# Another written-out order of steps in a fused recurrence and Fourier-mixing kernel

## The chip, the cores and the metric

The kernel runs on one core of one Trainium2 chip. The metric is the device time of the launch in microseconds; of the kernel before it is known from three runs and from one further profiled execution. The engines are named as in the profile: PE (TensorE, matmuls), PEld (its weight loads), DVE (VectorE), ACT (ScalarE), POOL (GpSimd) and SP (SyncE, here the issuer of nearly all DMAs). PSUM is the memory that PE writes.

## What is computed

Two blocks follow one another. The first is a gated linear recurrence over 768 tokens for 4 batches of 8 heads of width 48. The second mixes each batch's 768 x 384 matrix by a two-dimensional Fourier transform, normalises it, and passes it through two projections with a ReLU between them.

```python
f = 1.0 / (1.0 + np.exp(-f_logit))
for t in range(S):
    state = f[:, :, t, :, None] * state + np.einsum('bhd,bhe->bhde', k[:, :, t], v[:, :, t])
    y[:, :, t] = np.einsum('bhd,bhde->bhe', q[:, :, t], state)
x = y.transpose(0, 2, 1, 3).reshape(B, S, H * D)
u = x + np.real(np.fft.fft(np.fft.fft(x, axis=1), axis=2))
un = (u - mean(u)) / np.sqrt(var(u) + 1e-06)          # over the last axis
out = u + np.maximum(un @ w_ch1, 0.0) @ w_ch2          # 384 -> 1536 -> 384
```

## The kernel before

**Units.** The recurrence is cut into 16 units, one for each batch and pair of heads (`attention`, L316). Unit `u` belongs to batch `u // 4`. Each unit is a generator of 13 or 14 steps:

1. gates: two ACT passes over `g` (L331, L332)
2. the running sum of the log gates on DVE (`W`, L338), with two small operations (L339, and L340 on POOL)
3. three exponentials on ACT (L343, L344, L346)
4. `q` and `k` scaled on DVE (L350, L351)
5. scores `sc` on PE (L362): 24 matmuls on 48x64 tiles of the array, four tiles side by side, into two PSUM tiles
6. the causal mask on DVE (L369, two operations, one for each PSUM tile)
7. transposes `st` of the keys on PE (L507) and their copy `kT` on ACT (L509)
8. the states' increments `ds` on PE (L518, tiled)
9. the scan over chunks on DVE (L526)
10. `y` from the scores on PE (L538, tiled)
11. `y` from the states on PE (L545, tiled) and five copies `yT` on ACT (L554 to L558)
12. transposes `yt` back on PE (L565) and the copy into `x` on ACT (L567)
13. and 14. the fold of tokens and channels for the Fourier transform, on DVE and POOL (L591 to L614); step 14 exists for the last two units of a batch

**Batches.** When its four units are folded, a batch goes through `fnet`: four steps `z` (L652) with copies on ACT, then three steps `mix` (L671) with additions and moments on DVE. A further generator, `turns`, makes the normalised rows `un` (L707), their transposes `pt` (L710) and the copies `unT` (L711). `projected` then runs the first projection `up` (L752, 12 steps for each pair of row blocks, each followed by a ReLU on ACT, L754) and the second one, for the first pair as plain products `po` (L761), for the others as seven products of a Strassen-like scheme, `fx` and `fz` (L775), with additions on DVE (L782 to L809) and the stores of `out` (L619 on POOL's queue, L626 on SP's or ACT's).

**Weights.** The weights come as 64-bit words in 24 blocks. Each is fetched by SP (384 KB, L268), at most three ahead, and brought to single precision by one ACT, two DVE and one POOL operation (L239, L241, L242, L243). Later they are read a second time, and DVE takes each block's smallest size (L302). A last test, `judge`, combines these with the recurrence's extremes into one flag: six small DVE operations (L824 to L829), one matmul `turned` (L831), two more DVE operations (L832, L834). All engines load the flag (L884) and branch on it (L885); where it is set, which it is not for these inputs, everything is computed again in a slower way.

**The order.** No scheduler decides. The string `ORDER` lists 684 words, and each engine gets its instructions in this order, each engine's queue in program order. A number means that unit's next step. `F`, `H` and `P` with a number mean the next step of that batch's `fnet`, `turns` and `projected`. `L` loads gates, keys, queries or values of a unit (`L4fk`), `r` fetches a weight block, `R` three, `C` converts one, `W` makes the sums for the seven products, `V` reads a block again and `c` takes its size, `M` is the test. `D` puts four matmuls of constant data on PE (L154) that keep it occupied. `G` clears the middle rows of a tile, `I`, `i`, `T`, `S`, `Z` set up constants and tables.

**Buffers.** `sc` (two tiles), `st`, `ds` and `yt` share one PSUM pool of two buffers; `z`, `mix`, `pt`, `up`, `po`, `fx` and `fz` share another of two; `y` has one. Gates and keys have three tiles, queries four, values four, raw weight blocks three.

Of the kernel before, what the change touches and what calls it, by code (L numbers as in the profile page):

```python
# [12 lines left out]
C = 128  # L13
# [11 lines left out]


ORDER = (
    "Gq2 r I D Gq0 L0f Gk1 L1f D Gk0 L0q i D Gq3 C Gq1 Z L0k 0 D 1 Gk2 0 L1q 1 L1k D D D D D D D D D D D "
    "D 0 0 1 0 r 1 L2f 0 2 C L1v 1 L3fk 1 3 L0v 0 1 L2q 2 0 0 r 1 L2k 3 1 0 2 r 3 L3q 2 L2v 0 C L3v C "
    "L4fk R 4 2 2 3 1 0 C 2 4 1 3 L5qv D L4qv L5fk 3 D D 3 2 0 2 3 2 3 C r 4 1 4 L6fk C r 2 5 4 L6qv 4 2 "  # L30
    "1 5 6 3 4 D 4 C 5 3 T 3 6 4 5 5 4 2 r L7fk 5 2 D L7qv 3 3 5 7 S L8fk C 4 7 6 6 5 F0 5 r r F0 F0 F0 "
    "7 4 C F0 L9fk 5 6 8 H0 H0 6 5 6 r H0 C L8qv 6 7 L9qv P0 6 7 r C P0 7 7 C 9 P0 r r 5 8 C r C F0 r 7 "
    "F0 6 P0 5 9 C 6 7 P0 r C P0 8 8 C P0 r r 7 P0 P0 8 9 H0 C P0 P0 8 7 8 C P0 H0 7 9 6 H0 H0 C 9 r C "
    "P0 9 L10fk r 9 P0 r C 9 L11fk 10 C 6 6 P0 11 4 P0 P0 P0 P0 P0 P0 10 P0 P0 P0 L10qv P0 P0 7 7 F1 9 "
    "P0 F1 H0 9 W P0 P0 P0 11 F1 P0 L11qv P0 P0 P0 9 P0 P0 P0 8 L12fk P0 11 11 8 P0 P0 10 11 F1 P0 11 11 "
    "10 L14fk F1 8 P0 14 F1 P0 10 P0 8 10 P0 P0 H1 H1 10 L12qv P0 P0 10 P0 F1 P0 11 11 10 P0 10 H1 P0 P0 "
    "P0 P0 12 12 12 P0 P0 12 P0 H1 P0 12 P0 H1 L13fk P1 P1 P1 P1 P1 14 13 P1 12 8 8 P1 P1 12 9 10 L13qv "
    "13 P1 P1 L14qv 9 P1 12 11 P1 H1 11 10 P1 P1 13 P1 13 P1 12 P1 P1 14 P1 14 V 13 P1 c V 10 10 P1 P1 "
    "P1 P1 P1 V L15fk P1 13 P1 11 V P1 P1 P1 P1 c P1 11 11 F2 V c F2 F2 H1 13 H1 F2 c 14 P1 c V c P1 P1 "
    "12 P1 P1 14 P1 P1 13 V V V P1 15 F2 c P1 12 P1 P1 P1 P1 c P1 H2 14 15 V V P1 P1 P1 P1 P1 13 P1 14 "  # L40
    "F2 P1 c P1 P1 15 V 13 P1 H2 P1 P1 L15qv P1 14 13 P1 V 12 H2 F2 14 P2 P2 P2 P2 P2 P2 P2 15 P2 P2 P2 "
    "c c 12 H2 V H2 15 H2 15 P2 c P2 15 P2 P2 15 P2 14 13 15 P2 P2 14 P2 P2 15 13 P2 P2 P2 P2 P2 H2 V 15 "
    "P2 P2 14 14 15 H2 P2 P2 P2 P2 15 15 F3 F3 P2 F3 F3 P2 F3 c P2 P2 P2 P2 P2 V P2 c P2 V c c V P2 P2 "
    "P2 P2 P2 c P2 F3 F3 P2 V P2 H3 P2 P2 P2 H3 H3 P2 P2 P2 P2 P2 P2 P2 P2 P2 P2 P3 H3 c P3 P3 P3 P3 V "
    "P3 c P3 P3 P3 c V V c P3 P3 P3 H3 P3 P3 P3 P3 P3 P3 c P3 P3 V P3 H3 P3 P3 P3 P3 P3 P3 H3 H3 P3 P3 "
    "P3 P3 P3 P3 P3 P3 P3 P3 P3 P3 V P3 P3 P3 P3 P3 c P3 c P3 P3 P3 M P3 P3 P3 P3 P3 P3 P3 P3 P3 P3 P3 "
    "P3"
)

PAIRS = ((0, 3), (2, 5), (1, 4))  # L50
# [4 lines left out]
def kernel(  # L55
# [14 lines left out]
    B, HP, _, D, _, S = qkf.shape  # L70
# [8 lines left out]
    R = 64 + D  # L79
# [417 lines left out]
    def outputs(u, x_all, AT, Q, K, te, T=None):  # L497
# [66 lines left out]
        for c, i in enumerate((0, 1, 4, 2, 3, 5)):  # L564
# [4 lines left out]
            ps[:, :NCH * 128].rearrange("t (c r k) -> t c r k", r=2, k=64)[:, :, :, :D])  # L569
        yield  # L570
        yield from fold(u, x)

    eo_of = {}

    def fold(u, x):

        b, hp = divmod(u, HP)
        if b not in eo_of:
            eo_of[b] = p1.tile([128, 8, DM], F32, tag="eo", name=f"eo{b}")
        eo = eo_of[b] if hp < HP - 1 else eo_of.pop(b)
        ch = slice(hp * 2 * D, (hp + 1) * 2 * D)
        f = eo[:, :, ch]
        last = hp == HP - 1
        other = nc.vector if last else nc.gpsimd  # L590
        other.tensor_tensor(f[:, 6:3:-1], x[:, 0:3, ch], x[:, 3:6, ch], ALU.subtract)  # L591
        nc.vector.tensor_tensor(f[:, 1:4], x[:, 0:3, ch], x[:, 3:6, ch], ALU.add)
        nc.vector.tensor_tensor(f[:, 0:8:7], f[:, 1:7:5], f[:, 2:6:3], ALU.add)
        nc.vector.tensor_tensor(f[:, 2:6:3], f[:, 1:7:5], f[:, 2:6:3], ALU.subtract)
        other.tensor_copy(f[:, 1:7:5], f[:, 0:8:7])
        other.tensor_copy(f[0:1, 0], f[0:1, 2])
        other.tensor_tensor(f[0:1, 2:7:4], x[0:1, 0:2, ch], x[0:1, 3:5, ch], ALU.subtract)
        if hp < HP // 2:
            return
        yield  # L600


        lo, hi = (QD + 1, HD) if hp == HP // 2 else (1, QD + 1)
        up = slice(DM - lo, DM - hi, -1)
        tt = nc.vector.tensor_tensor
        tt(xs[:, :, lo:hi], eo[:, 4:7, lo:hi], eo[:, 4:7, up], ALU.subtract)
        if last:
            tt(se[:, :, 1:QD], xs[:, :, 1:QD], xs[:, :, HD - 1:QD:-1], ALU.subtract)
            tt(xs[:, :, 1:QD + 1], xs[:, :, 1:QD + 1], xs[:, :, HD - 1:QD - 1:-1], ALU.add)
        tt(xc[:, :, lo:hi], eo[:, 0:4, lo:hi], eo[:, 0:4, up], ALU.add)  # L610
        if last:
            nc.vector.tensor_copy(xc[:, :, 0:HD + 1:HD], eo[:, 0:4, 0:HD + 1:HD])
            tt(ce, xc[:, :, 0:QD + 1], xc[:, :, HD:QD - 1:-1], ALU.add)
            tt(xc[:, :, 0:QD], xc[:, :, 0:QD], xc[:, :, HD:QD:-1], ALU.subtract)  # L614
# [362 lines left out]
```

## Time and profile before

| what | value |
|---|---|
| median of 3 runs | 552.56 us (552.45 to 554.12) |
| span of the profiled execution | 551.2 us |
| PE, DVE, ACT, POOL busy | 527.8, 300.1, 192.8, 96.1 us |
| `up` L752 on PE | 864 matmul passes, 197.0 us |
| `fx` and `fz` L775 on PE | 161.8 us in all forms |
| `sc`, `y`, `y`, `ds` (L362, L538, L545, L518) on PE | 26.3, 55.0, 21.4, 32.3 us |
| DMA | 44.38 MB, mean 81 GB/s |

The profiled execution is 1.3 us shorter in its span than the runs' median; the runs' time also counts what lies around the span. PE's busy time counts matmuls that overlap, so it says where PE works and not how fast. A matmul in single precision appears as two passes in the trace, so that `up`'s 12 steps of three matmuls appear as 72 passes. L154, the constant matmuls, take 12.9 us of PE's busy time in the first 65 us.

### The profile page before, as it was taken

To read this page: it belongs to the slowest core of one execution; us is meant where nothing else is said; L and a number is where in the kernel's file an instruction comes from. 1 tells how busy PE (TensorE), PEld (TensorE's weight loads), DVE (VectorE), ACT (ScalarE), POOL (GpSimd) and SP (SyncE) were. 2 spreads that over 40 slices of the span, in tenths; PEclk is the share of its full clock that TensorE was granted. 3 is DMA by queue.
4 is the path that set the end of the run, shared out by engine and by line. 5 is a ranking of instruction groups with operands and counts; after the bars stand their busy time and mean duration, and the time that the engine had idled before them with its cause. 6 is when DMAs were issued, how large, how long until landed. Compare 5 with 4: busy or idle time off the path is not lost.

```text
span 551.2 us, 10204 instructions
## 1 busy us (share of the span) xinstructions
PE 527.8 (96%) x4186; PEld 463.6 (84%) x4186; DVE 300.1 (54%) x534; ACT 192.8 (35%) x497; POOL 96.1 (17%) x147
## 2 busy tenths in 40 slices
PE   7797989999999999999999999999999999999995
PEld 5686768876898889889889899899889798989985
DVE  8999999984936437426644344444452441413231
ACT  5767485771332432551340422321411303021110
POOL 7146535434001000121101001003001000010000
PEclk9888799999999999999999999999999999999999
DMA  8979745353102100412540301002012004000001
GB/s 220 260 212 227 210 136 165 122 175 107 51 0 73 44 1 7 111 44 84 160 115 17 114 1 59 29 1 87 0 30 87 1 14 159 0 30 0 30 2 34
DMA packets 18398, 44.38 MB, mean 81 GB/s; under 512 B 3109, under 2 KB 4710, under 8 KB 18342
## 3 DMA queue, kind: packets, MB, share of 16 engines
q1 hardware_dynamic: 17094, 39.89, 25.9%
q0 software_dynamic: 1104, 3.54, 1.8%
q8 instruction: 35, 0.57, 0.4%
q10 hardware_dynamic: 144, 0.20, 0.1%
q14 instruction: 21, 0.17, 0.1%
HBM read 38.90 MB, written 4.72 MB: 79 GB/s over the span
## 4 chain that ended last, share of the span: by engine, by line
PE 88%; DVE 3%; ACT 3%; DMA 2%; POOL 1%; issue 1%; SPq 0%; ACTq 0%; POOLq 0%
PE up L752 35%; PE fx L775 16%; PE fz L775 12%; PE y L538 4%; PE sc L362 3%; PE z L652 3%; PE y L545 3%; PE po L761 3%; PE mix L671 3%; PE ds L518 2%; PE yt L565 2%; PE st L507 1%; PE pt L710 1%; DMA k<-in_qkf_dram 1%; DMA g<-in_qkf_dram 1%
## 5 line engine op out<-in xcount | busy, mean ns | idle before, releaser
L752 PE MATMUL up<-unT,w 128*128 128x256 f32 x864 | 197.0, 382 | 1.5 <-DVE x L730 0.9
L752 PEld LDWEIGHTS up<-unT,w 128*128 128x128 f32 x864 | 161.0, 190 | 26.1 <-issue 1.5
L754 ACT ACTIVATE h<-up 128x256 f32<-128x256 f32 x144 | 55.2, 383 | 199.4 <-PE up L752 199.4
L619 POOL DMA_INDIRECT out_dram<-x,place x16 | 16.9, 1056 | 270.4 <-DVE x L805 234.0
L775 PE MATMUL fx<-block,h 128*128 128x192 f32 x264 | 46.5, 326 | 0.0
L775 PE MATMUL fx<-w,h 128*128 128x192 f32 x264 | 44.9, 327 | 0.1
L775 PEld LDWEIGHTS fx<-w,h 128*128 128x128 f32 x264 | 43.1, 190 | 0.8 <-ACT h L754 0.4
L775 PEld LDWEIGHTS fx<-block,h 128*128 128x128 f32 x264 | 43.5, 190 | 0.0
L782 DVE TENSOR_TENSOR s<-h,h 128x768 f32<-128x768 f32 x11 | 10.5, 954 | 50.3 <-ACT h L754 50.3
L243 POOL TENSOR_TENSOR w<-w,raw 128x384 uint32<-128x384 uint32 x24 | 28.2, 1178 | 45.8 <-ACT raw L239 25.6
L369 DVE COPY_PREDICATED at<-causal,sc 128x768 f32<-128x768 uint32 x32 | 31.3, 1031 | 0.9 <-PE sc L362 0.8
L362 PE MATMUL sc<-q,W 48*64 48x128 f32 x768 | 26.3, 283 | 5.2 <-issue 3.3
L362 PEld LDWEIGHTS sc<-q,W 48*64 48x64 f32 x768 | 22.1, 138 | 8.9 <-issue 5.4
L338 DVE TENSOR_TENSOR_SCAN W<-g,bound 112x768 f32<-112x768 f32 x16 | 28.4, 1775 | 0.8 <-issue 0.7
L727 DVE TENSOR_TENSOR x<-mix,x 128x384 f32<-128x384 f32 x12 | 6.7, 555 | 39.0 <-PE mix L671 39.0
L538 PE MATMUL y<-at,v 128*64 128x128 f32 (+1 forms) x384 | 27.9, 300 | 0.0
L538 PEld LDWEIGHTS y<-at,v 128*64 128x64 f32 (+1 forms) x384 | 23.9, 143 | 3.2 <-issue 3.2
L775 PE MATMUL fz<-w,s 128*128 128x192 f32 x132 | 23.5, 328 | 0.0
L775 PE MATMUL fz<-block,h 128*128 128x192 f32 x132 | 23.5, 328 | 0.0
L775 PE MATMUL fz<-w,h 128*128 128x192 f32 x132 | 23.4, 327 | 0.0
L775 PEld LDWEIGHTS fz<-w,s 128*128 128x128 f32 x132 | 21.6, 190 | 0.3 <-issue 0.3
L697 ACT ACTIVATE rstd<-mv,eps 128x1 f32<-128x1 f32 (+1 forms) x20 | 5.9, 294 | 45.7 <-DVE mv L694 45.7
(145 smaller groups left out, 750.3 us busy)
## 6 DMA issues: line engine op xcount, KB each, us to landing
raw<-in_w_ch_dram SPq DMA_DIRECT2D x24, 384.0 KB, 4.3
g<-in_qkf_dram SPq DMA_DIRECT2D x32, 144.0 KB, 4.4
q<-in_qkf_dram SPq DMA_DIRECT2D x32, 144.0 KB, 4.1
k<-in_qkf_dram SPq DMA_DIRECT2D x32, 144.0 KB, 4.7
v<-in_v_dram SPq DMA_DIRECT2D x16, 288.0 KB, 5.0
k<-in_w_ch_dram SPq DMA_DIRECT2D x12, 384.0 KB
g<-in_w_ch_dram SPq DMA_DIRECT2D x12, 384.0 KB, 5.2
out_dram<-x SPq DMA_DIRECT2D x4, 168.0 KB
```

The costliest lines, as they stand in the source:

```text
L243: nc.gpsimd.tensor_tensor(bits, bits, lo, ALU.add)
L338: nc.vector.tensor_tensor_scan(W, g, bound[:R], 0.0, ALU.add, ALU.min)
L362: nc.tensor.matmul(ps[64 * s:64 * s + 64, r, i * C:(i + 1) * C], lhsT=W[ROWS[r], o + 64 * s:o + 64 * s + 64], rhs=Q[ROWS[r], o:o + C], sta ...
L369: nc.vector.copy_predicated(AT[:, :, half], causal.bitcast(U32).unsqueeze(1).unsqueeze(1).to_broadcast([128, 2, NCH // 2, C]), ps[:, :, :N ...
L538: nc.tensor.matmul(y[FILL[r], c * C:(c + 1) * C], lhsT=vt[:, c, r * D:r * D + (64 if r == 0 else D)], rhs=AT[:, r, c], start=(c % 4 == 0), ...
L545: nc.tensor.matmul(y[ROWS[r], c * C:(c + 1) * C], lhsT=st[ROWS[r], :, c - 1], rhs=Q[ROWS[r], c * C:(c + 1) * C], start=False, stop=True, s ...
L619: nc.gpsimd.indirect_dma_start(out=out.rearrange("b s d -> (b s) d"), out_offset=bass.IndirectOffsetOnAxis(ap=place[:, b, i:i + 1], axis=0 ...
L652: nc.tensor.matmul(z[:, cols], lhsT=src[:, j, lo:hi], rhs=tab[:, t, T % 2, cols], start=(i == 0), stop=(i == len(parts) - 1), skip_group_c ...
L671: nc.tensor.matmul(mix[:, o], lhsT=zz[:rows_of[T], T, PLACES[c]], rhs=cd[:rows_of[T], T, :NQ - odd], start=(i == 0), stop=(i == 1))
L752: nc.tensor.matmul(pp[:, :256], lhsT=w1[:, kt, m * 128:(m + 1) * 128], rhs=unT[:, kt], start=(kt == 0), stop=(kt == 2))
L754: nc.scalar.activation(hs[-1][:, m % H].rearrange("p t n -> p (t n)"), pp[:, :256], AF.Relu)
L775: nc.tensor.matmul(out, lhsT=h[:, m], rhs=blocks[i][:, m], start=(start and m == 0), stop=(m == H - 1), skip_group_check=True)
```

## The change

The list of words is another one. Each word stands in it as often as before. What differs is their sequence: tiled steps of several units stand next to each other, the first loads and the clearing of tiles come in another order, the weight blocks are fetched and converted at other places, `up` and product steps stand between the units' steps in another way, and the test `M` is the last word, where twelve words `P3` followed it before.

Where the two lists have reached the first `P0`, the word counts are these: the old one has done 11 `C` and the steps of unit 5 up to 11, unit 6 up to 8, unit 7 up to 4 and unit 8 up to 1; the new one has done 8 `C` and the steps of unit 5 up to 12, unit 6 up to 4 and unit 7 up to 3. Units 0 to 3 and unit 4 up to step 12 are done in both, and all 21 `D`.

A second edit keeps a batch's fold buffer in the table until the last step that uses it, so that the last steps of a batch's units may come in another sequence.

The diff, with the list cut to its start and its end:

```diff
 ORDER = (
-    "Gq2 r I D Gq0 L0f Gk1 L1f D Gk0 L0q i D Gq3 C Gq1 Z L0k 0 D 1 Gk2 0 L1q 1 L1k D D D D D D D D D D D "
-    "D 0 0 1 0 r 1 L2f 0 2 C L1v 1 L3fk 1 3 L0v 0 1 L2q 2 0 0 r 1 L2k 3 1 0 2 r 3 L3q 2 L2v 0 C L3v C "
...
-    "P3 P3 P3 P3 P3 P3 P3 P3 P3 P3 V P3 P3 P3 P3 P3 c P3 c P3 P3 P3 M P3 P3 P3 P3 P3 P3 P3 P3 P3 P3 P3 "
-    "P3"
+    "I L0f D Gq2 D Gq3 Gk2 D D Gq0 Gq1 L1f D Gk1 Gk0 0 D 1 0 D D Z L2f L0q D L0k 0 L1k D i D L0v 1 D D 0 "
+    "L1q D 0 L1v L2q 1 2 0 r 0 1 0 0 D 2 L2k 1 1 D 0 2 2 L3fk 1 L4fk 1 C 3 1 0 L3q 2 3 L2v 2 4 3 1 L4qv 2 "
+    "1 0 L5fk 2 1 3 4 D 2 D 5 L3v 3 0 4 3 2 D L5qv 4 3 r 2 5 3 L7fk D 3 r 4 3 1 C 5 4 3 r 5 C 3 4 L6fk 4 "
+    "3 2 4 D T 2 5 5 7 C 4 2 S 6 4 5 R L6qv 3 6 7 4 F0 L8fk F0 C F0 C r L7qv F0 5 5 6 F0 5 5 H0 H0 r C r "
...
+    "13 P0 10 12 10 H1 11 12 13 L15fk F1 P1 13 9 V 10 12 12 11 12 L14fk 10 P1 P1 F1 13 L14qv H1 10 13 11 "
...
+    "P3 V P3 P3 V P3 P3 P3 P3 c P3 P3 P3 P3 P3 P3 P3 V P3 P3 P3 P3 P3 c c P3 M"
 )
@@ fold
-        eo = eo_of[b] if hp < HP - 1 else eo_of.pop(b)
+        eo = eo_of[b]
...
         if last:
+            eo_of.pop(b)
             tt(se[:, :, 1:QD], xs[:, :, 1:QD], xs[:, :, HD - 1:QD:-1], ALU.subtract)
```

## The prediction

> **What bounds the kernel now.** I read the page first (shares, slices, chain), then the chain of waits piece by piece, then the first 84 us in stretches with VectorE's waits, and last the instructions at the end. The page:
>
> ```profile
> PE 527.8 (96%) x4186; PEld 463.6 (84%) x4186; DVE 300.1 (54%) x534; ACT 192.8 (35%) x497; POOL 96.1 (17%) x147
> ...
> PE   7797989999999999999999999999999999999995
> ...
> DVE  8999999984936437426644344444452441413231
> ...
> PE 88%; DVE 3%; ACT 3%; DMA 2%; POOL 1%; issue 1%; SPq 0%; ACTq 0%; POOLq 0%
> ```
>
> The reader is to see two stages. From the seventh slice on TensorE is at 9 everywhere and the chain runs along it. In the first six it is not, while VectorE is at 8 or 9. The first 84 us in stretches (PE, PEld, DVE, ACT, POOL busy, then clock, DMA share, GB/s):
>
> ```profile
> 0.00:10.00 10.00, 6.07 (x32) 4.44 (x33) 7.66 (x11) 5.38 (x8) 8.13 (x23) 1.00 0.83 206
> ...
> 20.00:30.00 10.00, 8.17 (x148) 7.16 (x148) 9.15 (x14) 7.43 (x15) 1.08 (x3) 0.84 1.04 266
> ...
> 70.00:84.00 14.00, 12.41 (x158) 9.80 (x159) 13.36 (x24) 11.32 (x37) 3.37 (x5) 1.00 0.56 156
> ```
>
> VectorE is busy for 78.0 of 84 us and its waits sum to 3.7 us: this stage is VectorE's. It ends with the first `up` matmul at 83.78, the first step P0, because from there TensorE always has projection work to fall back on. The chain of waits from there:
>
> ```profile
> 83.78 1.49 PE up L752 x6
> 85.27 1.47 PE sc L362 x48
> 86.74 1.49 PE up L752 x6
> 88.23 0.48 PE st L507 x5
> 88.72 1.31 PE up L752 x6
> ```
>
> Six `up` matmuls take 1.31 us behind the full-array step `st` and 1.49 behind `sc`, which works in quarters of the array (48x64 tiles). Reading each piece's start to the next start between 150 and 540 us: six `up` take 1.30 after full-array work, 1.40 where a tiled step comes before or after, 1.49 with one on both sides. So a visit to the tiled steps (`sc`, `ds`, `y` L538, `y` L545) costs 0.19 us on the full-array work beside it, and nothing shows between two tiled steps: `ds` hands over to `y` in 0.01 to 0.08 us.
>
> The end of the run, in order of time (start, duration, instruction):
>
> ```profile
> 525.80 0.28 DVE L832 TENSOR_REDUCE most<-turned 1x1 f32<-1x128 f32 x1 [8.30 <-PE turned L831]
> ...
> 545.06 0.56 DVE L809 TENSOR_TENSOR x<-fx,x 128x384 f32<-128x384 f32 x1 [1.59 <-PE fx L775]
> 546.54 0.38 ACTq L626 DMA_DIRECT2D out_dram<-x  x1
> ```
>
> and the register load of the test's flag (L884) and the branch on it (L885), durations in ns, first and last start:
>
> ```profile
> L884 SPq TENSOR_LOAD <-flag x1: 471/471/471, 526.3 to 526.3; - x1
> ```
>
> ```profile
> L885 SPq EVENT_SEMAPHORE  x8: 17/17/17, 529.6 to 549.5; - x8
> ...
> L885 SPq COMPARE_BRANCH  x1: 50/50/50, 527.1 to 527.1; - x1
> ```
>
> The last VectorE operation ends at 545.62, the span 5.6 us later. The test (step M) is written and loaded by SP at 526, far ahead; SP then takes 2.4 us from its branch (527.1) to its next instruction (529.6), hidden here.
>
> **What the Trainium skill says.** "TensorEngine Tiling (Array Packing)", Key Properties, says that changing the tiling mode, not just the tile, drains TensorE; the trace agrees and prices it at 0.19 us a visit. "TensorE: Matmul & The Clock Gate", Part 1, says that the array's clock drops to half after an idle window and comes back after a busy one; the trace agrees: its clock record has four stretches of half clock, 17 us in all, between 20 and 64 us, and none from there to the end of the work. "Perfetto Trace Analysis" (its opening) says that matmul busy time is a bad metric because matmuls are pipelined; so I use starts of pieces, not the 96%.
>
> **The change part by part.** Both lists have 684 steps, each name equally often, so nothing is computed less; the `pop` moved in the fold only lets the units of a batch finish in another sequence.
>
> *1. The first stage.* Up to the second `un` (L707), which the first `up` needs, VectorE's list loses three weight blocks (L241, L242: 10 becomes 7, 3 x (0.443+0.570) = 3.0 us), one pair L350/L351 (0.975+1.054 = 2.0) and two L369 (2 x 1.031 = 2.1): 7.1 us less. The rest is the same set of operations. If VectorE idled as little as now, the first `up` would come at 83.78 - 7.1 = 76.7. I walked the first 22 us by hand: the first gate load no longer stands behind a 384 KB weight block, so the first scan starts about 1.4 us earlier than 8.11, but it waits 0.8 us for the gates, and 0.8 us for the first scores, since unit 1's products (step 4) come behind unit 0's mask. Later the Fourier step F0 has 7 us of VectorE work beside 8 us of TensorE work, another 1 us. About 2 us more idle time than before, so a gain of 5.1. Bounds: 7.1 with no more idle time, and zero, or a loss of a microsecond, if loads or half clock leave VectorE 7 or 8 us more.
>
> *2. TensorE's work from the first P0 on.* One `sc` (1.28), `st` (0.48) and `ds` (0.59) more remain to be done then, and one `yt` (0.58) and `mix` (1.31) less: +0.5 us.
>
> *3. Tiled steps side by side.* From the first P0 on, 38 tiled steps stand in 37 visits in the old list, and 40 in 19 visits in the new one: 18 x 0.19 = 3.4 us off TensorE, which is the bound. Nothing covers this, so it comes in full.
>
> *4. New waits on TensorE.* I laid TensorE's pieces one behind another and looked at the work between maker and user: a mask needs 2.3 us behind `sc` (two L369 at 1.03 and a handover), `kT` 0.85, the scan L526 0.95, the copies `yT` 1.75. From the first P0 on the old list is short at two places (0.4 and 0.15 us), the new one at four: 0.1, 0.5 (unit 11's `y` behind unit 10's), 0.5 (unit 10's `yt` behind unit 12's scores), 0.02. VectorE's backlog behind TensorE after the first P0 comes to about 3 us by my sum, where it came to 5 before with 1.2 us of gaps in the trace, so I take +0.5. The queues: SP loads in this order wait for tiles that are free by then, and weight blocks are still fetched up to three ahead (POOL's add, 1.18 us each, is spread wider). I cost both at nothing; the cover is projection work.
>
> *5. The test M moves behind the last P3.* Gone from the middle are the matmul `turned` and the gap behind it (0.54 + 0.2): -0.7. At the end, counted from the end of L809: six small operations to L829 (0.9), the matmul and its handover (0.5), L832 and L834 (0.5), so the flag at +1.8. Then SP: load, register step and branch 0.9, instruction fetch 2.4, eight semaphore steps 0.5, the last wait list (549.54 to 550.35 in this trace) 0.8, final barrier 0.9: 7.3 us in place of 5.6, so +1.7. The bounds: +1.0, if the fetch is shorter on a queue that had nothing else to do; +2.8, if POOL's branch (2.6 us fetch, then 2.5 us of draining) ends last. I take +1.9.
>
> Sum: -5.1 + 0.5 - 3.4 + 0.5 - 0.7 + 1.9 = -6.3 us. The profiled span is 551.2, so 544.9; the runs' median is 552.56 (1.3 above the span), so 546.3.
>
> **The rivals.**
>
> *A, no gain in the first stage* (loads, not VectorE, set it: the DMA share is 1.04 in four of the stretches up to 60 us, and the first TensorE steps fall into half clock). Against it: VectorE waits for a load nowhere in the 84 us. Then the sum is -1.2: 551.4.
>
> *B, the full gain* (VectorE as dense as before, the fetch at the end partly hidden, no new gaps): -7.1 + 0.5 - 3.4 - 0.7 + 1.0 = -9.7: 542.9.
>
> *C, slower: the tiled steps side by side wait.* Scores, `st`, `ds` and `yt` share two PSUM buffers of one pool, so a step that follows closely waits for a copy by VectorE or ScalarE. 21 tiled steps follow another directly now. If each waits half a mask copy, 0.5 us, that is 10.5 us: 556.8. It decides from 6.3 / 21 = 0.3 us each. Against it: neighbours are mostly steps of different units, and the distances in 4 are short only at four places; for it: those distances assume that VectorE has reached the step, which it has not in the first 40 us after P0.
>
> That the change doesn't do what it says is excluded by the counts in 3.
>
> **How the numbers follow.** Likeliest case 0.52, A 0.16, B 0.16, C 0.16. A change within 0.3% (1.7 us) can't be told from none here. The likeliest and B are faster; of A about 0.06 is faster, 0.08 within the bound and 0.02 slower; C is slower. So faster 0.74, same 0.08, slower 0.18. The range runs from B with a little more, 542, to A with the longer ending, 553, and leaves out most of C.
>
> **What would show it.** Right: the first `up` near 78 to 79 us; `up` pieces of 1.30 where pieces of 1.49 stood, and the whole work from first `up` to the last L809 about 3 us shorter than 461.3; 7 us or so between L809's end and the end of the span, with L832 inside. Wrong: VectorE waits for TensorE or loads by over 8 us before the first `up`; gaps before `sc`, `st`, `ds` or `yt` in the middle that sum to over 4 us.

## The result, and the profile after

The new list took 549.73 us (median of 4 runs, 549.3 to 550.58), the old one beside it 553.23 us (4 runs, 552.45 to 554.12): a ratio of 0.9942, with an interval from 0.9926 to 0.9958. The change makes the kernel 0.6% faster, about half of the 1.1% that was forecast. The profiled span went from 551.2 to 547.7 us, by 3.5. The page of the kernel after:

```profile
PE 516.8 (94%) x4186; PEld 457.4 (84%) x4186; DVE 303.7 (55%) x534; ACT 192.0 (35%) x497; POOL 91.9 (17%) x147
...
PE   7897889998999999999999999999999999999993
...
DVE  7999999988745267554641563537063230414132
...
PE 79%; DVE 13%; ACT 2%; issue 2%; POOL 1%; DMA 0%; DVEq 0%; POOLq 0%; ACTq 0%
```

Three things are to be seen. DVE's count of instructions is the same as before (534), but its busy time is 3.6 us longer: the same operations ran longer. On the chain of waits DVE has 13%, where it had 3%. And PE's last slice is at 3 instead of 5: more time after its last work.

Where the time went is easiest to read at four moments that both lists pass. They divide the 3.5 us into parts:

| us | before | after | difference |
|---|---|---|---|
| first `up` on PE | 83.7 | 75.7 | -8.0 |
| last `po` starts | 134.6 | 130.3 | -4.3 |
| first `up` of batch 1 | 221.0 | 214.8 | -6.2 |
| last L809 ends | 545.6 | 538.9 | -6.7 |
| end of the span | 551.2 | 547.7 | -3.5 |

The first `up` comes 8 us earlier, which is 3 more than forecast. But of these 8 us, 3.7 are lost again before the last `po`, and 3.2 behind the last L809; the work between these two moments is 2.4 us shorter. The stage between first `up` and last `po`, in stretches (PE, PEld, DVE, ACT, POOL busy with instruction counts, then clock, DMA share, GB/s):

```profile
75.65:90.00 14.35, 12.69 (x104) 10.69 (x103) 14.11 (x20) 8.81 (x19) 5.58 (x5) 1.00 0.71 192
90.00:100.00 10.00, 8.84 (x152) 7.59 (x152) 9.72 (x20) 6.50 (x18) 4.07 (x4) 1.00 0.56 160
100.00:110.00 10.00, 9.34 (x123) 8.10 (x120) 9.59 (x14) 7.59 (x16) 5.25 (x5) 1.00 0.70 192
110.00:120.00 10.00, 9.54 (x84) 6.12 (x83) 9.86 (x15) 6.20 (x15) 4.75 (x5) 1.00 0.75 204
120.00:130.00 10.00, 9.12 (x28) 4.97 (x27) 7.51 (x14) 0.00 (x0) 5.70 (x11) 1.00 0.44 122
```

In the kernel before, two of the same stretches read:

```profile
90.00:100.00 10.00, 10.00 (x101) 8.49 (x100) 9.58 (x20) 6.49 (x19) 6.73 (x7) 1.00 0.39 122
110.00:120.00 10.00, 10.00 (x113) 7.97 (x112) 9.87 (x15) 6.67 (x18) 4.03 (x4) 1.00 0.51 151
```

After the change PE is busy for less than the whole of every stretch; before, it was busy for the whole of each one from 83.78 to 140. DVE is nearly full up to 120 us in both kernels. Before, it kept up and PE lacked nothing; after, it is behind, and PE waits for it. So DVE goes on setting the pace for some 45 us beyond the first `up`. What PE waits for between 75.65 and 140 us (total, times, longest):

```profile
PE st L506 <- DVE at L368: 1.6, 2, 1.2
PE up L752 <- DVE x L765: 1.5, 1, 1.5
PE sc L361 <- DVE W L350: 0.9, 1, 0.9
PE po L761 <- POOL w L242: 0.9, 2, 0.6
PE sc L361 <- PE up L752: 0.7, 1, 0.7
PE yt L564 <- DVE at L368: 0.3, 1, 0.3
PE up L752 <- DVE x L730: 0.3, 1, 0.3
```

They sum to 6.2 us; the same view of the kernel before, from 83.78 to 140, lists none. From 140 us on the sums are 1.5 before and 0.7 after, so the new list's waits from the first `up` on are 5.4 us more. A sum says the same: from the first `up` to that of batch 1 PE takes 137.3 us before and 139.1 after, though it has less to do there (two `mix`, one `yt` and one `pt` less, one `st` and one `ds` more: -2.5) and 11 visits fewer to the tiled steps (11 x 0.19 = 2.1); 139.1 - (137.3 - 4.6) = 6.4 us are lost, by estimate. (Up to L605 a line number of the kernel after is one less than before: L241 and L242 there are the DVE and POOL operations that were L242 and L243.)

Why DVE is late shows in its own instructions (start, duration, instruction):

```profile
108.91 0.56 DVE L241 SCALAR_TENSOR_TENSOR w<-raw,w 128x384 uint32<-128x384 uint32 x1
109.38 0.36 DVE L240 TENSOR_SCALAR w<-raw 128x384 uint32<-128x384 uint32 x1
109.77 1.26 DVE L241 SCALAR_TENSOR_TENSOR w<-raw,w 128x384 uint32<-128x384 uint32 x1
```

and POOL's in the same microseconds:

```profile
109.60 1.01 POOL L242 TENSOR_TENSOR w<-w,raw 128x384 uint32<-128x384 uint32 x1 [0.69 <-ACT g L342]
```

The first L241 takes 0.56 us. The second begins at 109.77, while POOL's addition for the block before it is running (109.60 to 110.61), and ends at 111.03, 0.42 us after POOL. All ten L241 that begin during an addition end 0.41 or 0.42 us behind it. The L240 shown, with one input, keeps its 0.36, but it begins before the addition. One that begins during an addition is held up too, as the same operation shows in the kernel before:

```profile
110.28 1.01 POOL L243 TENSOR_TENSOR w<-w,raw 128x384 uint32<-128x384 uint32 x1 [2.51 <-ACT raw L239]
110.58 0.94 DVE L241 TENSOR_SCALAR w<-raw 128x384 uint32<-128x384 uint32 x1
```

It takes 0.94 us in place of 0.35 and ends 0.22 us after the addition. The Trainium skill, "SBUF — State Buffer", section "Who interferes with whom", says that a DVE instruction with two inputs in SBUF contends with a GpSimd instruction that reads SBUF, and that the one that comes second is blocked until the first has finished. The lines of L241 in the kernel after agree with that, but for a little: 0.42 us behind the addition is less than the 0.56 that the operation takes alone, so some 0.14 us of it pass while it is held. The causal mask L368, whose second input is in PSUM, takes 1.07 us at most, beside POOL or not.

In the new list the words `C` stand in pairs or a step or two apart while DVE is the bound, so that one block's addition on POOL meets the next block's L241. I summed, for every DVE operation that overlaps one of POOL's, what it took beyond an undisturbed one of its form, where that was over 0.2 us. Up to the first `up` that is 4.6 us before and 3.9 after. From there to the last `po` it is 4.9 us in 8 operations before, and 9.5 us in 13 operations after. Of the 9.5, 5.6 are eight of the 24 L241 (two more of them are stretched ahead of the first `up`). Of the 4.9 before, 2.8 are operations with one full-size input, four of them L241 there. The new order changed which operations meet an addition.

The end of the run is the other loss. The last L809 ends at 538.86. The flag's load and the branch behind it, by queue (durations in ns, first and last start):

```profile
L885 SPq EVENT_SEMAPHORE  x8: 17/17/17, 544.8 to 545.4; - x8
L885 POOLq EVENT_SEMAPHORE  x5: 17/43/43, 544.4 to 544.7; - x5
...
L885 POOLq COMPARE_BRANCH  x1: 53/53/53, 541.3 to 541.3; - x1
L885 PEldq COMPARE_BRANCH  x1: 4462/4462/4462, 541.3 to 541.3; - x1
...
L885 SPq COMPARE_BRANCH  x1: 50/50/50, 541.6 to 541.6; - x1
```

and POOL's queue behind it:

```profile
L972 POOLq DRAIN  x3: 40/107/1467, 545.4 to 547.4; - x3
```

All five queues branch between 541.3 and 541.6. The first instruction behind the branch comes at 544.4 on POOL, at 544.8 on SP (3.3 us after its branch; before it was 2.5). POOL then has a semaphore step of 0.5 us and a DRAIN of 1.467, which ends at 546.86, last of all. Its DRAIN was 1.467 before, too.

### The profile page after: what moved, and what is told of

Read it like the earlier page. It is cut to its first block, busy times and chain, and to the rows that moved or that the text cites. A ratio compares the mean times of both kernels' runs of the same rounds, so it can differ in the third digit from the quotient of the medians.

```text
span 547.7 us, 10206 instructions
## 1 busy us (share of the span) xinstructions
PE 516.8 (94%) x4186; PEld 457.4 (84%) x4186; DVE 303.7 (55%) x534; ACT 192.0 (35%) x497; POOL 91.9 (17%) x147
## 4 chain that ended last, share of the span: by engine, by line
PE 79%; DVE 13%; ACT 2%; issue 2%; POOL 1%; DMA 0%; DVEq 0%; POOLq 0%; ACTq 0%
PE up L752 32%; PE fx L775 15%; PE fz L775 11%; PE z L652 4%; PE y L537 3%; PE y L544 3%; PE mix L671 3%; PE sc L361 2%; DVE w L241 2%; DVE at L368 2%; DVE W L337 2%; PE ds L517 1%; DVE W L350 1%; PE pt L710 1%; PE yt L564 1%
## 5 line engine op out<-in xcount | busy, mean ns | idle before, releaser
L752 PE MATMUL up<-unT,w 128*128 128x256 f32 x864 | 194.4, 380 | 2.7 <-DVE x L765 1.5
L752 PEld LDWEIGHTS up<-unT,w 128*128 128x128 f32 x864 | 161.9, 190 | 24.9 <-DVE x L765 1.9
L782 DVE TENSOR_TENSOR s<-h,h 128x768 f32<-128x768 f32 x11 | 10.5, 955 | 57.5 <-ACT h L754 57.5
L368 DVE COPY_PREDICATED at<-causal,sc 128x768 f32<-128x768 uint32 x32 | 31.3, 1034 | 13.6 <-PE sc L361 13.6
L242 POOL TENSOR_TENSOR w<-w,raw 128x384 uint32<-128x384 uint32 x24 | 27.7, 1154 | 35.7 <-ACT raw L238 13.1
L537 PE MATMUL y<-at,v 128*48 128x128 f32 (+1 forms) x384 | 24.6, 275 | 0.0
L537 PEld LDWEIGHTS y<-at,v 128*48 128x48 f32 (+1 forms) x384 | 21.2, 130 | 2.3 <-issue 2.0
L775 PEld LDWEIGHTS fz<-block,h 128*128 128x128 f32 x132 | 21.6, 190 | 0.5 <-PE fx L775 0.3
L775 PEld LDWEIGHTS fz<-w,h 128*128 128x128 f32 x132 | 21.8, 190 | 0.0
```

What stands on the lines that cost most here:

```text
L242: nc.gpsimd.tensor_tensor(bits, bits, lo, ALU.add)
L368: nc.vector.copy_predicated(AT[:, :, half], causal.bitcast(U32).unsqueeze(1).unsqueeze(1).to_broadcast([128, 2, NCH // 2, C]), ps[:, :, :N ...
L537: nc.tensor.matmul(y[FILL[r], c * C:(c + 1) * C], lhsT=vt[:, c, r * D:r * D + (64 if r == 0 else D)], rhs=AT[:, r, c], start=(c % 4 == 0), ...
L752: nc.tensor.matmul(pp[:, :256], lhsT=w1[:, kt, m * 128:(m + 1) * 128], rhs=unT[:, kt], start=(kt == 0), stop=(kt == 2))
L775: nc.tensor.matmul(out, lhsT=h[:, m], rhs=blocks[i][:, m], start=(start and m == 0), stop=(m == H - 1), skip_group_check=True)
```

## The experiments

Theory 1: the new list gains what was forecast in the first stage and by its tiled neighbours; the missing half is lost by DVE, which stays the bound for longer than assumed, and by the test at the end. The rivals: the first stage brings nothing of its own; the tiled neighbours bring nothing; one late piece of the order (a fold ahead of L765) makes the waits; the half clock of PE makes the difference. The times stand as medians, the ratios against the kernel before on the same chip.

**The test earlier in the new list.** The words `c c M` and one `V` go ahead of the last twelve `P3`.

```diff
-    "P3 V P3 P3 V P3 P3 P3 P3 c P3 P3 P3 P3 P3 P3 P3 V P3 P3 P3 P3 P3 c c P3 M"
+    "P3 V P3 P3 V V P3 P3 P3 P3 c P3 c c M P3 P3 P3 P3 P3 P3 P3 P3 P3 P3 P3 P3"
```

> The new list with the test M, the two sizes before it and the last rereading moved ahead of the last twelve P3. Theory 1 (the longer ending of 8.8 us in place of 5.6 is the test: flag, fetch on all queues, and POOL's 2.5 us of draining, all of which run beside the last products if the test is early): the ending returns to 5.6 us, the matmul of the test costs 0.65 us in the middle again, 549.7 - 3.2 + 0.65 = 547.1 us. Rival (POOL's draining of 1.5 us waits for the last stores and stays at the end): 548.6 us.

Measured: 547.19 us (546.9 to 548.36), ratio 0.9895 [0.9883, 0.9908]. The end behind the last L809 is 5.66 us again (8.84 in the kernel after, 5.60 before). This is what theory 1 said (547.1). Putting the test last costs 549.73 - 547.19 = 2.5 us in sum. This list leaves nothing out and is faster than both kernels.

**The test last in the old list.**

```diff
-    "P3 P3 P3 P3 P3 P3 P3 P3 P3 P3 V P3 P3 P3 P3 P3 c P3 c P3 P3 P3 M P3 P3 P3 P3 P3 P3 P3 P3 P3 P3 P3 "
-    "P3"
+    "P3 P3 P3 P3 P3 V P3 P3 P3 P3 P3 c P3 c P3 P3 P3 P3 P3 P3 P3 P3 P3 P3 P3 P3 P3 P3 P3 M"
```

> The old list with the test M as its last word and nothing else. Theory 1 (the ending is 8.8 us with the test behind the last product, whatever stands before): 553.1 + 3.2 - 0.65 = 555.7 us. My forecast's working (SP's chain alone) gives 553.1 + 1.7 - 0.65 = 554.2.

Measured: 556.51 us (555.03 to 557.83) against 552.72, ratio 1.0071 [1.0048, 1.0094]; the end behind the last addition is 9.04 us. That is 3.8 us slower, more than the 2.6 of theory 1 and far more than the 1.1 of the forecast's working. So the ending costs 3.2 to 3.4 us in either list. In the other profiles below that keep the test last it is 9.1 to 10.3 us long, so 8.84 is the shortest of them.

**The new front with the old rest**, joined at the first `P0`; and **the old front with the new rest from P1 on**. At each junction the words of the other list follow that had not yet been used.

```diff
-    "5 H0 C 7 6 F0 P0 C 8 6 P0 r C 6 P0 6 L8qv r C 7 P0 P0 8 r C P0 F0 P0 r 6 6 L9fk C r 6 7 8 r C 7 C 6 "
+    "5 H0 C 7 6 F0 C r r C L9fk 6 8 6 6 r C L8qv 6 7 L9qv P0 6 7 r C P0 7 7 C 9 P0 r r 8 C r C r 7 F0 6 "
```

> The new list up to its first P0, then every word that is left in the order of the old list, the test at its old place. The words that the old list does before its first P0 and the new one after it now stand before the first P0 again. Theory 1 (the new list reaches P0 8 us earlier because 7 us of VectorE work stand behind P0 in it; the way the first stage is interleaved brings only the rest): first up near 82.7 us, about 1 us off the kernel before, 552.2 us. Rival (the interleaving of loads, blocks and units is what gains): first up at 77 or earlier and 547 us or less.

> The old list up to its first P1, then the words left in the order of the new list, with the test ahead of the last twelve P3. From P1 on TensorE never waits long in either profile; there are 18 tiled steps in 9 visits in place of 17. Theory 1 (each visit saved is 0.19 us of TensorE time in full): 8 x 0.19 = 1.5 us off, 551.7 us. Rival (steps side by side wait for each other's PSUM buffers and give it back): 553.2 us or more.

Measured: 556.23 us, ratio 1.0058 [1.0045, 1.0071], and 566.76 us, ratio 1.0233 [1.0208, 1.0259]; both expectations missed. In the first one the first `up` comes at 86.4, later than before. What PE waits for between 60 and 100 us shows why:

```profile
PE st L506 <- DVE at L368: 3.4, 1, 3.4
PE sc L361 <- DVE W L350: 2.2, 1, 2.2
```

At the junction PE's steps come directly behind the DVE operations that they need; 10.2 us of half clock, from 79.2 us on, lie in the same place. In the second the junction makes one long wait, in PE's timeline:

```profile
233.84 1.38 PE L564 MATMUL yt<-ident,yT 112*128 112x112 f32 x6 [11.08 <-DVE at L368]
```

Two lists joined in this way have holes that neither list has. The two runs say little about the parts of the change; what they do show is that a single place where a step stands too close behind a mask can cost 11 us. In the second run 17.1 us of half clock follow from 227.2 us on, during and behind that wait, and add to its cost. I then changed single places of the new list only.

**Lighter weight blocks.** In the last 16 of the 24 blocks the two DVE operations are left out; the weights differ, the rest is the same.

```diff
+        if done[0] < 8:
-        nc.vector.tensor_scalar(bits, hi, 3, None, ALU.logical_shift_left)
-        nc.vector.scalar_tensor_tensor(bits, hi, 0x80000000, bits, ALU.bitwise_and, ALU.bitwise_xor)
-        nc.gpsimd.tensor_tensor(bits, bits, lo, ALU.add)
+            nc.vector.tensor_scalar(bits, hi, 3, None, ALU.logical_shift_left)
+            nc.vector.scalar_tensor_tensor(bits, hi, 0x80000000, bits, ALU.bitwise_and, ALU.bitwise_xor)
+        nc.gpsimd.tensor_tensor(bits, bits if done[0] < 8 else lo, lo, ALU.add)
```

> The new list, where the two VectorE operations (shift and sign) of the conversion are left out for the last 16 of the 24 weight blocks, so those weights are other numbers; POOL's addition stays. This takes 16 us from VectorE, nearly all of it between the first up and 120 us. Theory 1 (the 6 us of gaps on TensorE between 76 and 134 us come from VectorE being behind): the gaps vanish but for the 1.5 us before 133.6, the time is 4 to 5 us shorter, 545 us. Rival (the gaps come from steps standing side by side that wait for a buffer, whatever VectorE has to do): 549.2 us or more.

Measured: 546.15 us (544.89 to 546.44), ratio 0.9874 [0.986, 0.9889]. The first `up` is at 75.5, the last `po` starts at 125.3 in place of 130.3. Theory 1's 545 was a little too low, the rival's 549.2 is far off. So DVE, not PE's own work, holds up this stage: with less for DVE to do, 5 us of it go, and 3.6 of them reach the end.

**The fold behind L765 later.** PE's single longest wait in this stage is for L765 (1.5 us at 133.6). DVE reaches L765 behind the folds of units 4 and 5; two `P0` are drawn ahead of these.

```diff
-    "L10fk C C P0 6 P0 P0 9 4 L11qv 7 P0 L11fk 11 5 P0 P0 6 P0 P0 P0 P0 10 P0 P0 W 9 H0 P0 P0 7 P0 9 9 9 "
+    "L10fk C C P0 6 P0 P0 9 P0 P0 4 L11qv 7 L11fk 11 5 P0 6 P0 P0 P0 P0 10 P0 P0 W 9 H0 P0 P0 7 P0 9 9 9 "
```

> The new list with the end of the second plain product (its P0) and the one behind it moved ahead of the folds of units 4, 7 and 5 and two loads. Theory 1 (the addition L765 that frees the product's PSUM tile stands behind four folds on VectorE; TensorE waits 1.5 us at 133.6 us for it): the wait goes, 549.7 - 1.5 = 548.2 us. Rival (VectorE's folds are late in any case and what needs them waits instead): 549.7 us.

Measured: 558.17 us (557.61 to 558.81), ratio 1.0097 [1.0073, 1.0122], 8 us slower than the new list; neither expectation foresaw that. The wait for L765 is gone, but in PE's timeline stands

```profile
147.72 0.88 PE L710 MATMUL pt<-ident,un 128*128 128x128 f32 x3 [7.01 <-DVE un L707]
```

DVE runs out of work while it waits for the products, then does the folds and the four sums of `W` (1.35 us each), and only then the `un` that PE waits for. The same with **one `P0` drawn ahead**, in the list with the early test:

```diff
-    "L10fk C C P0 6 P0 P0 9 4 L11qv 7 P0 L11fk 11 5 P0 P0 6 P0 P0 P0 P0 10 P0 P0 W 9 H0 P0 P0 7 P0 9 9 9 "
+    "L10fk C C P0 6 P0 P0 9 4 L11qv 7 P0 P0 L11fk 11 5 P0 6 P0 P0 P0 P0 10 P0 P0 W 9 H0 P0 P0 7 P0 9 9 9 "
```

> The list with the early test, where only the last of the folds (unit 5's) and a load and gates step stand behind the P0 that ends the second plain product, so that VectorE always has folds to do until the product is there. Theory 1: the addition L765 comes 1 to 1.5 us earlier and no later operation moves, 547.2 - 1.1 = 546.1 us. Rival (as in the run with all folds later, un comes later and TensorE waits for it): 547.2 us or more.

Measured: 549.17 us (548.36 to 550.16), ratio 0.9927 [0.9909, 0.9944], 2 us slower than the list with the early test; the rival was right. The wait has only moved:

```profile
144.10 0.52 PE L710 MATMUL pt<-ident,un 128*128 128x128 f32 x3 [2.72 <-DVE un L707]
```

So both ways that were tried of drawing L765 forward moved the wait to `un`, which comes later on DVE then, and made it longer. Whether another order of these words would do better is open.

**Without the last seven D.** The constant matmuls of `D` keep PE occupied; the words from the 15th `D` on are left out.

```diff
-    "L1q D 0 L1v L2q 1 2 0 r 0 1 0 0 D 2 L2k 1 1 D 0 2 2 L3fk 1 L4fk 1 C 3 1 0 L3q 2 3 L2v 2 4 3 1 L4qv 2 "
+    "L1q D 0 L1v L2q 1 2 0 r 0 1 0 0 2 L2k 1 1 0 2 2 L3fk 1 L4fk 1 C 3 1 0 L3q 2 3 L2v 2 4 3 1 L4qv 2 1 0 "
...
```

> The new list without its last seven D (28 constant matmuls that keep TensorE occupied between 20 and 50 us); nothing else is left out. In the profiles the old list has 17 us of half clock before 64 us, the new one 3.4. Theory 1 (VectorE sets the first stage, TensorE's clock there hardly counts): more half clock, first up within 1 us, time within 1 us of 549.7. Rival (the full clock is a part of the new list's gain): 551 us or more.

Measured: 551.02 us (17 runs, 550.12 to 552.6), ratio 0.9963 [0.9952, 0.9974], so 1.3 us slower than the new list. That is the rival's number (551 or more), and the first `up` comes at 78.6 us in the profile, 3 us later than in the new list, where theory 1 allowed 1 us. So the clock cannot be ruled out as a part of the first stage's gain, of about 1.3 us. The run does not show it cleanly either: its profile was taken of the slowest of the 17 executions, and the 13.7 us of half clock in it (3.4 in the new list, 17.1 in the old) lie at 17 to 24 and 75 to 82 us, where lists with all `D` have some too, and not at 20 to 50 us, where the words were left out. Of the profile's 3.2 us over the new list, 1.5 lie behind the last L809.

**The tiled steps apart.** In the list with the early test, one `P1` or `P2` is put between two tiled steps at ten places behind the first `P1`, one of which is shown:

```diff
-    "13 P0 10 12 10 H1 11 12 13 L15fk F1 P1 13 9 V 10 12 12 11 12 L14fk 10 P1 P1 F1 13 L14qv H1 10 13 11 "
+    "13 P0 10 12 10 H1 11 12 13 L15fk F1 P1 13 9 V 10 P1 12 12 P1 11 12 L14fk 10 F1 13 L14qv H1 10 13 P1 "
...
```

> The list of the run with the early test, where from the first P1 on each pair of tiled steps that stand side by side has one later P step moved between them: 19 tiled steps in 19 visits in place of 9. Theory 1 (0.19 us a visit, on TensorE in full): 547.2 + 10 x 0.19 = 549.1 us. Rival (no such cost, or the waits of neighbours vanish with it): 547.2 us or less.

Measured: 553.25 us (14 runs, 552.82 to 554.69), ratio 1.0008 [0.9997, 1.002]: all that the new list had won is gone. The chain of the new list, and below it that of this run:

```profile
226.05 1.47 PE sc L361 x48
227.52 1.09 PE y L544 x20
228.61 6.67 PE up L752 x30
```

```profile
227.96 1.47 PE sc L361 x48
229.43 1.49 PE up L752 x6
230.92 1.15 PE y L544 x17
```

Six `up` between two tiled steps take 1.49 us; in the long piece of the new list they take 6.67 / 5 = 1.33. From the first `up` of batch 1 to the last L809 this run takes 331.0 us, the list with the early test 324.7: 6.3 more. Of these, 2.9 are three waits that the moved words made (`pt` for `un` 1.3, `fz` for `x` 0.9, `yt` for `yT` 0.7). The other 3.4 us, for ten visits, are 0.34 each, where theory 1 had 0.19 and no waits. The price of 0.19 was read on `up` alone. The tiled step gains too: `ds` takes 0.78 us to the next step's start where full-array work follows (six times in the kernel before) and 0.59 where a tiled step follows (three times after).

**Without POOL's addition.** Is it DVE's amount of work, or POOL's interference? In the last 16 blocks DVE keeps two operations of the same forms, and POOL's addition is left out; the weights lose their low bits there.

```diff
+        if done[0] >= 8:
+            upper(dst, hi)
+            return
         bits = dst.bitcast(U32)
```

> The new list, where for the last 16 of the 24 weight blocks POOL's addition of the low words is left out and VectorE's two operations (as many and as long as before) make the upper 32 bits alone, so those weights are cut in place of rounded. VectorE has exactly as much to do. In the profile of the new list ten of 24 L241 take 1.26 us in place of 0.56, each time with a POOL addition (L242) running, and in all VectorE's operations are stretched by 9.5 us between the first up and the end of the second product, 4.9 in the old list. Theory 1 (the two-operand operations of VectorE stand still while POOL adds, and this is what puts VectorE behind): L241 is 0.56 us everywhere, most of the 6 us of TensorE's gaps before 134 us go, the time falls about as far as with VectorE's operations left out, to 546 us. Rival (the stretched durations are an artefact of the record, and VectorE's own work is what counts): 549.2 us or more.

Measured: 545.98 us (545.09 to 548.06), ratio 0.9882 [0.986, 0.9905]. That is 3.8 us faster than the new list, as much as leaving out the DVE operations brought. The last `po` starts at 126.1, and between the first `up`, at 77.4, and 140 us one of PE's waits is left (L755 and L768 are L752 and L765 of the kernel after):

```profile
PE up L755 <- DVE x L768: 1.5, 1, 1.5
```

What DVE's operations take beyond their undisturbed time is 2.0 us in this stage, instead of 9.5. So DVE's own work can be done in time where no addition stretches it, and less work on DVE (the lighter blocks) does as well: what counts is when DVE is done. One rival isn't parted from this: without the addition a block is ready sooner, and 0.9 of the 6.2 us of PE's waits were `po` waiting for the addition itself.

**Both together**: the early test, and no addition in the last 16 blocks.

> The new list with the test early, and GpSimd's addition left out of the last 16 of the 24 weight blocks (their weights are cut to the upper 32 bits; VectorE's instructions stay as many). Theory 1 (GpSimd's additions hold up VectorE's two-input operations, and the test's place at the end is a cost of its own, so that both gains add): 547.2 - 3.8 = 543.4 us, between 542.8 and 544.2, with the first up at 77 to 78 us and the end 5.7 us behind the last L809. Rival (the two gains overlap, since what is won before 130 us only lets the list's end wait for loads, stores or the clock): 545 us or more.

Measured: 542.6 us (542.15 to 543.77), ratio 0.9827 [0.981, 0.9844], the first `up` at 75.7, the end 5.78 us behind the last L809. The two gains add to within a microsecond (543.4 was expected, 542.8 at the least). With the first `up` at the same moment as in the new list, PE's waits up to 140 us are 2.7 us in place of 6.2. It is no replacement for the kernel, since it drops low bits of two thirds of the weight blocks; it gives the size of what the additions cost, 547.19 - 542.6 = 4.6 us here.

## Why the prediction was right in direction and wrong in size

The direction was right; the size was not, above all in part 4. Step by step, on the profiled spans (in part 4, 5.4 is read from the waits, 4.9 is what the other lines leave of the sum):

| part | forecast | measured |
|---|---|---|
| 1 first stage | -5.1 | -8.0 |
| 2 work left after the first `up` | +0.5 | counts as forecast |
| 3 tiled steps side by side | -3.4 | at least as forecast where it could be read, see below |
| 4 new waits | +0.5 | +4.9 to +5.4 |
| 5 test: middle, end | -0.7, +1.9 | -0.7 taken, +3.2 |
| sum | -6.3 | -3.5 |

*Part 1* was too small. DVE's busy time up to the first `up` fell from 77.7 to 70.4 us (7.3; 7.1 was reckoned), and its idle time fell by 0.8 us, where 2 us more were assumed. The moment itself is a poor measure, though. Runs whose lists are the same up to the first `P0` put it anywhere between 75.5 and 78.3 us (with 3.4 to 10.2 us of half clock), and most of the difference was gone by the last `po` (130.3 after 75.7, 131.3 after 78.3). Where it came at 77.1 or later, a stretch of half clock began at 73.5 to 75 us; where it came at 75.7 or earlier, none lay there. So the gain over the old list's 83.7 is 5.4 to 8.2 us by run, and part of the 8.0 may be the luck of the profiled execution.

*Part 3* holds, as far as it could be read. From the first `up` of batch 1 on, where waits are few, the list with the early test takes 324.7 us and the old one 324.6, though the new one has one `sc` (1.47), one `mix` (1.31) and one `pt` (0.33) more to do there, 3.1 us in all. Its listed waits are 0.6 us shorter, so the eight visits fewer to the tiled steps (17 before, 9 after; 37 and 18 in all by the traces, where the prediction counted 37 and 19) save 2.4 us, 0.3 each, where the price of 0.19 gives 1.5. Pulling the steps apart gave 0.34 a visit. What the visits saved ahead of batch 1 (20 before, 9 after) can't be told from the waits there. Rival C put the waits at the tiled neighbours, at 10.5 us. In the chain above `y` follows `sc` with no gap, and the total excludes its 556.8. But what it said for itself, that DVE has not reached the step in the first 40 us after P0, is what happened: of the 6.2 us, 3.5 stand before `sc`, `st` and `yt`, and 2.8 of these end with a DVE operation.

*Part 4* is the step that failed. It said "VectorE's backlog behind TensorE after the first P0 comes to about 3 us by my sum" and took +0.5 us; of POOL's addition it said that it "is spread wider" and costed that at nothing. The durations that the prediction shows are means of the kernel before, in which L242 was hardly ever stretched (0.570 us); the same operation, L241 after, has a mean of 0.854. In the trace 13 operations were stretched by 9.5 us in this stage, 4.6 more than before, so by estimate the backlog is not 3 us but 3 + 4.6 = 7.6, more than the 5 of before. PE paid for it with 5 us of waits. Without the additions 3.8 us came back, and 4.6 in the list with the early test. The stage from the first `up` to the last `po` says the same in every profile: 50.8 to 50.9 us in the three with the old list there, 53.1 to 54.7 in the six with the new one or nearly so, 48.7 to 49.7 in the three where the additions or DVE's two operations are left out. What was moved out of the first stage, three blocks' conversion, was moved into a stage where DVE was also the bound and where blocks stood closer together: part of part 1's gain was only put off.

Part of it stays open: of the 4.9 to 5.4 us the additions account for 3.8 to 4.6, up to 0.9 of which are their own delay of `po`. The 1.5 us for L765 remain without them, and the attempts to mend it by order alone made it worse. The prediction's own sign of being right, 3 us less from the first `up` to the last L809, didn't come: 463.2 us, where the old list took 461.9.

*Part 5* was mis-sized by 1.3 us. The flag was ready 1.8 us behind L809, as reckoned. The forecast took SP's chain (+1.7 to +1.9) and named POOL's branch as the upper bound (+2.8), and this bound is what happened: POOL's queue ended last. Beyond it, POOL's queue took 3.1 us from its branch to its next instruction, not 2.6, and SP's 3.3, not 2.5, with all five queues branching within 0.3 us.

Rivals A (551.4) and B (542.9) fall with these numbers: the first stage did gain, by 5.4 us at the least, and B's "no new gaps" did not hold. The measured 549.73 is nearer to A's number than to the forecast's 546.3, though A's reason is wrong, so the time alone would not have told which part failed: 3 us more gain than forecast in part 1 hid the better part of the 4.4 to 4.9 us of part 4.

## What to carry to other kernels

Where work is moved out of a stage bound by one engine, ask first whether that engine is still the bound where the work arrives; if so, the gain is put off and not made. Sum an engine's backlog with the durations that it will have beside its neighbours in the new order, not with those of the old one: here a DVE operation that began during one of POOL's additions took about twice its time (0.56 became 1.26, 0.95 became 1.77), so look which operation will meet each addition. And a last test that all queues branch on is better placed ahead of the last work: here that was worth 2.5 us for one line of the list.

## What the runs showed of the hardware that was not expected

- A DVE operation that starts while one of POOL's additions runs is held until the addition is over. With two inputs in SBUF: 1.26 us instead of 0.56 (L241, ending 0.41 us after the addition), 1.77 instead of 0.95 (L350, 0.81 us after). With one input, in the kernel before: L241 at 110.58 took 0.94 and at 101.42 1.18 instead of 0.35, L707, with one full-size input, 1.20 instead of 0.47 (each ending 0.22 us after the addition). The mask L368 kept its 1.01 to 1.07 beside additions, and an operation that had begun before the addition kept its time (L240 at 0.36). POOL is held in the same way: two additions that began during a DVE operation with two inputs took 1.78 and 1.52 us instead of 1.01 (at 100.41 beside L525, at 117.47 beside L350), and two L240 that fell into this waiting kept their 0.35.
- From the branch to the next instruction SP took 2.5 to 2.7 us in the seven profiles where it branched ahead of the others, and 3.3 to 3.6 in the six where five queues branched within 0.3 us; POOL took 2.6 to 2.9 and 3.1 to 3.7. The Trainium skill, "Runtime: NRT & Kernel Launch", section "Instruction fetch mechanics", says that a taken branch out of the current pages forces a fetch before execution can go on. The trace agrees: between 541 and 545 us its DMA view lists five transfers of kind `instruction`, and in the kernel before one between SP's branch and its next instruction. Why it takes longer when all queues do it at once is not shown.
- POOL's DRAIN at the end takes 1.467 us in all thirteen profiles, whether the test stands last or not, so here its length doesn't depend on the work before it.
